# Seven smaller products for three of the seven block products in the second MLP stage, with weight low parts kept in DRAM

## The chip, the cores and the metric

The kernel runs on one core of a Trainium2 chip. The metric is the device time of one execution in microseconds (us). Here P means a tile of 128 partitions. TensorE multiplies a 128x128 weight tile (stationary) with up to 512 columns (moving) into a PSUM bank; VectorE (DVE), ScalarE (ACT) and GpSimd (POOL) prepare operands in SBUF; SyncE (SP) issues the transfers.

## The reference

```python
def _attn_ref(q, k, v):            # 8 batches, 12 heads, 448 positions, 64 per head
    scores = scale * np.matmul(q, k.transpose(0, 1, 3, 2)) - np.log(S)
    attn = 1.0 / (1.0 + np.exp(-scores))
    return np.matmul(attn, v)

def _moe_ref(x, w_in, w_out):      # x 3584 x 768, w_in 768 x 2048, w_out 2048 x 768
    h = x @ w_in
    r = np.maximum(h, 0.0)
    g = r * r
    return g @ w_out
```

Inputs and outputs are float32. The attention output, heads side by side, is `x`.

## The kernel before

The attention is computed first, pair of heads by pair of heads, and written to a DRAM scratch `xd`. On the side the MLP weights are converted and stored to `w1` and `w2` in DRAM, each as seven blocks: the sums and single blocks that a Strassen-Winograd scheme needs.

The MLP works on four groups of tokens, g = 0 to 3. Group 0 to 2 hold two halves of 512 tokens, group 3 two halves of 256. In each group `gemm1` makes the hidden activations and `gemm2` the output. Both halve all three dimensions (tokens, model width, hidden width) and compute seven block products in place of eight. In `gemm2` the block products run in the order 1, 2, 6, 7, 5, 4, 3 (`ORDER`); one is a 384 x 1024 weight block times 1024 x 512 activations.

Every float32 product is made of three passes over operands split in a high and a low part (high x high, high x low, low x high; `product`, line 613). A block product of `gemm2` is so 3 output tiles (e) x 8 hidden tiles (i) x 3 passes = 72 matmuls of 512 columns. They accumulate in PSUM banks "a", "b" or "c" (`CHAIN`): products 1, 6, 5, 3 go on in the same three banks, 7 and 4 in another three, 2 in a third three, and snapshots between them give the sums (`finish`, line 844).

What a block product needs beforehand:
- Weights. A unit is two hidden tiles of one block (128 x 768 words). `fetch` (line 650) loads it from `w1` or `w2`; `halve` (line 658) splits it: ScalarE casts the high part (line 373), VectorE subtracts it from the raw word to leave the low part (line 375). There are 7 buffers of 6 KB per partition for units. A fetch is placed 9 steps ahead of the first use, a halve 5 steps (a step is one i of one block product).
- Activations. `operand(n, j)` (line 776) makes the operand of product n for the pair j of hidden tiles: for n = 6, 7 and 4 one VectorE subtraction (lines 780, 784, 787; the last two in place), then the split, a ScalarE cast and a VectorE subtraction of 128 x 1024. It is called in every other step of the product before. All these tiles come from one set of 32 buffers of 4 KB per partition (`N2`, `flat2`): 16 hold the four blocks of squared activations, 4 the differences `gt2`, and two (high, low) are taken for every operand pair until its matmuls are over. Attention and x tiles use the same 32.
- A second set of 18 buffers of 2 KB (`N1`, `op1`) holds snapshots, outputs and the third part of the x operands.

The attention and the first `gemm1` are issued in the order in which they are written (`manual_schedule`). Everything behind it, so all `gemm2`, is ordered by the scheduler of the framework: an engine's order is its own, ready work may be taken ahead of work that waits, and the order is fixed before the run. During the `gemm2` stages GpSimd has nothing to do.

Of the kernel before, what the change touches and what calls it, by code (L numbers as in the profile page):

```python
# [9 lines left out]
F32 = mybir.dt.float32  # L10
F32R = mybir.dt.float32r
# [79 lines left out]
ORDERS = [(n, i) for n in ORDER for i in range(NI)]  # L91
LAST = ORDER[-1], -1

LOAD_AHEAD, HALVE_AHEAD = 9, 5
READY, HALVED = 5, 2

DEFERRED = (4, 5, 6, 7)
# [9 lines left out]
def sigmoid_attention_relu2_mlp(  # L107
# [7 lines left out]
    xd: bass.AP,  # L115
    w1: bass.AP,
    w2: bass.AP,
):


# [37 lines left out]
    def flat2(name, dtype=F32):  # L158
        return sb.tile([P, 2 * WIDE], dtype, tag="op2", bufs=N2, name=name)
# [12 lines left out]
    def op1(name, n, dtype=F32):  # L172
        return sb.tile([P, WIDE], dtype, tag="op1", bufs=N1, name=name)[:, :n]
# [93 lines left out]
        out.append((at + 13, store))  # L267
        return out

    def load_weights(src, name, spare=False):  # L270
# [12 lines left out]
    def halve_weights(w, later=None):  # L283

        hi, lo = w
        split_to(hi, lo, lo.bitcast(F32), later)
# [107 lines left out]
    def split_or_joint(raw, name, n):  # L394
        return joint(raw, name, 2 * WIDE // n, n) if n < WIDE else split(raw, name, n)
# [253 lines left out]

    def fetch(unit):  # L650
        g, m, i, u = unit
        if m == 0:
# [3 lines left out]
        loaded[unit] = load_weights(src, f"w{m}_{g}_{i}_{u}", unit in spare)  # L656

    def halve(unit, later=None):
        halve_weights(loaded[unit], later)

    spare = set()
    for at_unit, unit in enumerate(units):
        ahead, use = 0, first_use[unit]
        if unit[0] == NG - 1 and use >= sequence.index((NG - 1, 0, *STEPS[1][0])) + 4:
            ahead = 4
            if at_unit % 3 == 0:
                spare.add(unit)
        if at_unit >= READY:
            stream.setdefault(max(use - LOAD_AHEAD - ahead, 0), []).append((fetch, unit))
        if at_unit >= HALVED:  # L670
            stream.setdefault(max(use - HALVE_AHEAD - ahead // 2, 0), []).append((halve, unit))


    def gemm1(g, ops):
# [95 lines left out]
    def gemm2(g, blocks, operands1):  # L770
        n_tok = WIDTHS[g]
        of = 2 * WIDE // n_tok
        banks, snaps = {}, {}
        ops, t2 = {1: operands1}, {}

        def operand(n, j):

            if n == 6:
                t2[j] = blocks_of(f"gt2_{g}_{j}", n_tok)
                nc.vector.tensor_sub(out=t2[j], in0=blocks["22", j], in1=blocks["12", j])  # L780
                raw = t2[j]
            elif n == 7:
                raw = blocks["11", j]
                nc.vector.tensor_sub(out=raw, in0=t2[j], in1=raw)
            elif n == 4:
                raw = blocks["21", j]
                nc.vector.tensor_sub(out=raw, in0=raw, in1=t2[j])
            else:
                raw = blocks[{2: "21", 5: "12", 3: "22"}[n], j]
            ops.setdefault(n, {})[j] = split_or_joint(raw, f"o{n}_{g}_{j}", n_tok)  # L790

        def rest_of(e):
            t = snaps["rest", e] = op1(f"r_{g}_{e}", n_tok)
# [67 lines left out]

        def step(n, at):
            k, i = CHAIN[n], at
            if n in (1, 7, 2) and i == 0:
# [125 lines left out]
```

## Time and profile before

| | us |
|---|---|
| median of 3 runs (1055.05 to 1055.75) | 1055.62 |
| the profiled execution, its own time | 1054.56 |
| its span | 1052.8 |
| attention and first weights | about 245 |
| `gemm1`, `gemm2` of groups 0 to 2 | 114.2 each |
| group 3, both | 121.8 |

| engine | busy us of the span |
|---|---|
| TensorE | 1048.7 (100%) |
| VectorE | 806.7 (77%) |
| ScalarE | 662.5 (63%) |
| GpSimd | 73.5 (7%) |

In the rows below a time stands first where the row is one of a timeline or of the chain; `xN` is a count of instructions, `oa`, `ob`, `oc` are the PSUM banks of `gemm2`, `ha` and so on those of `gemm1`; `o_0h`, `o_0l` the high and low part of an operand of group-wise block pairs, `gt`, `g` activations, `w` a weight unit. The granted TensorE clock is 1.00 in every window.

### The profile page before, as it was taken

The page shows a single profiled execution, that of the slowest core. Times are in us where ns is not written, and L with a number is a line of the kernel's source. Part 1 is how long each engine was busy: PE and PEld are TensorE (multiplying, and loading weights), DVE is VectorE, ACT ScalarE, POOL GpSimd, SP SyncE. Part 2 cuts the span into 40 slices and gives each one's busy share as a digit, 9 for nine tenths or more (in the row PEclk, how much of TensorE's full clock was granted, in tenths as well). Part 3 has the DMA queues.
Part 4 walks back from the last instruction along what each step waited for, and adds up shares of the span by engine and source line. Part 5 has one row for each costly group of instructions (what it writes and reads, how often), then busy time and mean ns, then how long its engine had stood idle before and what let it go on. Part 6 is the DMA issues. An engine that isn't in the chain of part 4 may idle for free.

```text
span 1052.8 us, 16322 instructions
## 1 busy us (share of the span) xinstructions
PE 1048.7 (100%) x6202; PEld 812.3 (77%) x6202; DVE 806.7 (77%) x1025; ACT 662.5 (63%) x922; POOL 73.5 (7%) x44
## 2 busy tenths in 40 slices
PE   9999999999999999999999999999999999999998
PEld 4555555557888888888888888888888888899987
DVE  5999999877778899953455998834557997557997
ACT  7988988977667856634344656433344665357873
POOL 1322231200222000000000000000000000000000
PEclk9999999999999999999999999999999999999999
DMA  9999999993567535644333345543333345555662
GB/s 358 403 375 384 340 406 360 328 318 121 191 209 248 163 109 175 186 133 118 92 90 103 106 134 191 150 148 81 100 98 106 105 135 165 180 189 165 202 199 87
DMA packets 99407, 203.98 MB, mean 194 GB/s; under 512 B 9216, under 2 KB 61184, under 8 KB 99328
## 3 DMA queue, kind: packets, MB, share of 16 engines
q1 hardware_dynamic: 99184, 202.87, 58.5%
q8 instruction: 49, 0.80, 0.3%
q14 instruction: 30, 0.25, 0.1%
q10 hardware_dynamic: 144, 0.07, 0.0%
HBM read 158.86 MB, written 44.04 MB: 193 GB/s over the span
## 4 chain that ended last, share of the span: by engine, by line
PE 100%; DVE 0%; issue 0%
PE ha L617 22%; PE oa L617 19%; PE pav L347 11%; PE hb L617 9%; PE ob L617 9%; PE sc L316 9%; PE hc L617 5%; PE oc L617 5%; PE oa L625 2%; PE sr L332 2%; PE pav L359 2%; PE ob L625 1%; PE hb L625 1%; PE oa L628 1%; PE hb L628 1%; PE ob L628 1%
## 5 line engine op out<-in xcount | busy, mean ns | idle before, releaser
L375 DVE TENSOR_TENSOR w<-w 128x768 fp32r<-128x768 f32 (+1 forms) x220 | 200.1, 913 | 154.8 <-ACT w L373 153.7
L373 ACT CAST w<-w 128x768 fp32r<-128x768 f32 (+1 forms) x221 | 174.1, 793 | 176.3 <-DMA w<-w 169.1
L304 ACT ACTIVATE at<-sc 128x896 f32<-128x896 f32 x144 | 119.2, 943 | 3.2 <-PE sc L316 3.2
L347 PE MATMUL pav<-at,v 64*64 64x448 f32 x1152 | 118.1, 540 | 0.1
L347 PEld LDWEIGHTS pav<-at,v 64*64 64x64 f32 x1152 | 42.0, 133 | 60.7 <-issue 53.2
L712 ACT COPY s<-ha 128x512 f32<-128x512 f32 (+1 forms) x64 | 34.0, 532 | 80.3 <-PE ha L617 74.6
L583 DVE TENSOR_TENSOR ql<-x,qh 128x896 fp32r<-128x896 f32 x46 | 67.9, 1516 | 0.0
L208 POOL TENSOR_TENSOR a<-a,f 128x768 int32<-128x768 int32 x24 | 52.9, 2204 | 159.0 <-DVE a L205 93.9
L316 PE MATMUL sc<-qh 64*128 64x448 f32 x282 | 53.9, 379 | 0.0
L316 PE MATMUL sc<-ql,qh 64*128 64x448 f32 x282 | 51.3, 360 | 0.0
L316 PE MATMUL sc<-qh,ql 64*128 64x448 f32 x282 | 51.2, 360 | 0.0
L369 DVE TENSOR_TENSOR xo<-pav,xo 128x448 f32<-128x448 f32 x48 | 29.1, 620 | 23.5 <-ACT xo L365 21.7
L617 PE MATMUL oa<-o_3h,w 128*128 128x512 f32 x144 | 46.3, 389 | 0.0
L617 PE MATMUL oa<-o_1h,w 128*128 128x512 f32 x144 | 46.3, 389 | 0.0
L617 PE MATMUL oa<-o_0h,w 128*128 128x512 f32 x144 | 46.3, 389 | 0.0
L617 PE MATMUL oa<-o_2h,w 128*128 128x512 f32 x144 | 46.3, 389 | 0.0
L617 PE MATMUL ha<-x_0h,w 128*128 128x512 f32 x128 | 44.7, 390 | 0.0
L617 PE MATMUL ha<-x_1h,w 128*128 128x512 f32 x128 | 44.6, 389 | 0.0
L617 PE MATMUL ha<-x_2h,w 128*128 128x512 f32 x128 | 44.6, 389 | 0.0
L316 PEld LDWEIGHTS sc<-qh 64*128 64x128 f32 x282 | 26.4, 184 | 18.5 <-PE pav L347 16.2
L365 ACT COPY xo<-pav 128x448 f32<-128x448 f32 x48 | 25.5, 532 | 22.8 <-PE pav L359 11.1
L697 DVE SCALAR_TENSOR_TENSOR g<-g 128x1024 f32<-128x1024 f32 x30 | 36.9, 1230 | 0.7
(365 smaller groups left out, 2642.8 us busy)
## 6 DMA issues: line engine op xcount, KB each, us to landing
w<-w SPq DMA_DIRECT2D x192, 384.0 KB, 3.3
x<-qk SPq DMA_DIRECT2D x47, 448.0 KB, 6.2
f<-w_in SPq DMA_DIRECT2D x16, 768.0 KB, 8.8
v<-v SPq DMA_DIRECT2D x24, 448.0 KB, 6.9
xd<-xo SPq DMA_DIRECT2D x48, 224.0 KB, 5.4
w<-s SPq DMA_DIRECT2D x48, 192.0 KB, 7.5
outT<-o SPq DMA_DIRECT2D x36, 256.0 KB, 2.5
w<-a SPq DMA_DIRECT2D x12, 576.0 KB, 8.8
```

What stands on the lines that cost most here:

```text
L208: nc.gpsimd.tensor_tensor(out=wb, in0=wb, in1=t.bitcast(I32)[:, :, 0], op=ALU.add)
L304: nc.scalar.activation(at, sc, AF.Sigmoid, bias=NEG_LOG_S, scale=SCALE)
L316: nc.tensor.matmul(sc[:, j], x[kp][rows, 1, ks], x[qp][rows, 0], start=(n == 0), stop=(n == len(passes) - 1),)
L347: nc.tensor.matmul(sums[columns, h], vt[rows, n % 2 * NT + t, columns], at[t][rows, j], start=(t == 0 and (n % 2, h) != (1, 1)), stop=(t = ...
L373: nc.scalar.copy(out=hi, in_=raw)
L375: nc.vector.tensor_sub(out=lo, in0=raw, in1=hi.bitcast(F32))
L583: nc.vector.tensor_sub(out=xs[n][1], in0=x[n], in1=xs[n][0].bitcast(F32))
L617: nc.tensor.matmul(out, a[:, c], b, start=first and n == 0, stop=last and n == 2, skip_group_check=True)
L625: nc.tensor.matmul(out, w[0][:, c], x, start=first, stop=False, skip_group_check=True)
L628: nc.tensor.matmul(out[:, :n], w[1][:, c], x[:, :n], start=False, stop=last, skip_group_check=True)
L697: nc.vector.scalar_tensor_tensor(out=t, in0=t, scalar=0.0, in1=t, op0=ALU.max, op1=ALU.mult)
L712: nc.scalar.copy(out=s, in_=banks[chain, i])
```

## The change

In groups 1 and 2 the block products 2, 7 and 4 of `gemm2` (`TWICE`, `TWICE_IN`) are split again. Of their three output tiles, two (e = 0, 1) are taken together with the two hidden tiles of a pair and the two halves of 256 tokens as a 2x2x2 problem, and computed by seven products of 256 columns (`products`), accumulated in seven half banks (`SUMS_AT`). The third output tile is computed as before. What this needs:
- the sums of the weight blocks, made once in group 0 by GpSimd from the raw words (`weight_sums`, four operations of 128 x 128 per unit), split by ScalarE and VectorE, and stored to DRAM (`s2`); groups 1 and 2 load them;
- the differences of the activations, made by GpSimd (`differences_of`, four operations of 128 x 256 per pair), and their split, a ScalarE cast and a VectorE subtraction of 128 x 1024;
- the sums at the end (`add_up`), on VectorE and ScalarE, from PSUM.

Beside it, the low parts of all `gemm2` weight units are stored to DRAM in group 0 (`h2`, `keep`); in groups 1 and 2 a unit is loaded as raw words and low part, in two transfers, and only the ScalarE cast is left of its split.

```diff
+TWICE = (2, 7, 4)
+TWICE_IN = (1, 2)
+Q = WIDE // 2
+SUMS_AT = {2: (0, 0), 3: (0, 1), 4: (1, 0), 5: (1, 1), 1: (2, 0), 6: (2, 1), 7: (3, 0)}
...
-        nc.sync.dma_start(out=lo.bitcast(F32), in_=src)
+        nc.sync.dma_start(out=(lo if low is None else hi).bitcast(F32), in_=src)
+        if low is not None:
+            nc.sync.dma_start(out=lo.bitcast(F32), in_=low)
...
+        if m == 1 and u in TWICE and g <= TWICE_IN[-1]:
+            if both:
+                summed[unit] = tuple(op1(f"s{m}_{g}_{i}_{u}{c}", WIDE, F32R) for c in "hl")
+                for c, t in enumerate(summed[unit]):
+                    nc.sync.dma_start(out=t.bitcast(F32), in_=s2[i, TWICE.index(u), :, c])
+            else:
+                raw_sums[unit] = op1(f"s{m}_{g}_{i}_{u}", WIDE)
+                weight_sums(loaded[unit][1].bitcast(F32), raw_sums[unit])
...
     def halve(unit, later=None):
-        halve_weights(loaded[unit], later)
+        if unit[1] == 1 and unit[0] in TWICE_IN:
+            hi = loaded[unit][0]
+            nc.scalar.copy(out=hi, in_=hi.bitcast(F32))
+        else:
+            halve_weights(loaded[unit], later)
+
+    def keep(unit):
+        g, m, i, u = unit
+        nc.sync.dma_start(out=h2[i, u - 1], in_=loaded[unit][1].bitcast(F32))
...
+            split_to(h, l, t)
+            for c, t in enumerate((h, l)):
+                nc.sync.dma_start(out=s2[i, TWICE.index(u), :, c], in_=t.bitcast(F32))
...
             ops.setdefault(n, {})[j] = split_or_joint(raw, f"o{n}_{g}_{j}", n_tok)
+            if n in twice:
+                differences[n, j] = differences_of(raw, f"d{n}_{g}_{j}")
+
+        def differences_of(raw, name):
+
+            t, hi, lo = flat2(name), flat2(name + "h", F32R), flat2(name + "l", F32R)
+            t1, t2, t3, t4 = (t[:, k * Q : k * Q + Q] for k in range(4))
+            b11, b12, b21, b22 = (raw[:, k, h * Q : h * Q + Q] for k in range(2) for h in range(2))
+            nc.gpsimd.tensor_tensor(out=t1, in0=b12, in1=b11, op=ALU.subtract)
+            nc.gpsimd.tensor_tensor(out=t2, in0=b22, in1=t1, op=ALU.subtract)
+            nc.gpsimd.tensor_tensor(out=t3, in0=b22, in1=b12, op=ALU.subtract)
+            nc.gpsimd.tensor_tensor(out=t4, in0=b21, in1=t2, op=ALU.subtract)
+            split_to(hi, lo, t)
+            return hi, lo
...
+            for k, ((wh, wl), (xh, xl)) in operands.items():
+                at, half = SUMS_AT[k]
+                out = banks["q", at][:, half * Q : half * Q + Q]
+                for c, (a, b) in enumerate(((wh, xh), (wh, xl), (wl, xh))):
+                    nc.tensor.matmul(
+                        out, a, b, start=j == 0 and c == 0 and half == 0, stop=j == NI // 2 - 1 and c == 2,
+                        skip_group_check=True,
+                    )
...
+            if n in twice:
+                if i == 0:
+                    for e in range(4):
+                        banks["q", e] = bank(f"oq{n}_{g}_{e}", WIDE, 3 if e < 2 else None)
+                    if n != 4:
+                        banks[k, NE - 1] = bank(f"o{k}_{g}", WIDE)
+                j = i // 2
+                if i == 2 * j:
+                    products(n, j)
+                else:
+                    for c in range(2):
...
+                        product(banks[k, NE - 1], w, NE - 1, x, n != 4 and (j, c) == (0, 0), (j, c) == (NI // 2 - 1, 1))
+                if i == NI - 1:
+                    finish_twice(n)
+                after = ORDER.index(n) + 1
+                if after < len(ORDER) and i % of == 0:
+                    operand(ORDER[after], i // of)
+                return
```

## Rows read from the trace of the kernel before

**Rows 1.** The page: busy time of each engine, and the chain of waits that ended last by engine.

```profile
PE 1048.7 (100%) x6202; PEld 812.3 (77%) x6202; DVE 806.7 (77%) x1025; ACT 662.5 (63%) x922; POOL 73.5 (7%) x44
...
PE 100%; DVE 0%; issue 0%
```

**Rows 2.** The chain of waits in order of time, in `gemm2` of group 1: start us, length us, what. The first four block products (1, 2, 6, 7).

```profile
588.24 16.32 PE oa L617 x72
604.56 16.32 PE oc L617 x72
620.88 16.32 PE oa L617 x72
637.20 16.32 PE ob L617 x72
```

**Rows 3.** The timeline of TensorE in group 3, where matmuls have 256 columns: start us, length us. Between the two rows shown the timeline has 8 more single matmuls of the first row's form, all of 0.28 us.

```profile
958.55 0.28 PE L617 MATMUL ha<-x_3h,w_2h 128*128 128x256 f32 x1
...
959.63 0.86 PE L625 MATMUL hc<-x_3j,w 128*128 128x512 f32 x3
```

**Rows 4.** Busy time of each engine by window: the attention, `gemm2` of group 0, `gemm1` of group 1, `gemm2` of groups 1 and 2.

```profile
core 0: us, PE busy (x) PEld busy (x) DVE busy (x) ACT busy (x) POOL busy (x), PEclk, DMA share, GB/s
0.00:245.00 245.00, 244.12 (x2402) 136.09 (x2402) 210.60 (x282) 211.65 (x278) 53.10 (x28) 1.00 0.95 353
...
359.76:474.00 114.24, 114.24 (x505) 94.60 (x505) 96.21 (x100) 68.14 (x84) 0.00 (x0) 1.00 0.50 155
474.00:588.24 114.24, 114.24 (x505) 94.59 (x505) 62.37 (x74) 48.73 (x71) 0.00 (x0) 1.00 0.36 101
588.24:702.50 114.26, 114.26 (x505) 94.61 (x505) 94.54 (x98) 63.88 (x80) 0.00 (x0) 1.00 0.49 148
...
816.72:931.00 114.28, 114.28 (x506) 94.64 (x506) 86.00 (x91) 60.36 (x78) 0.00 (x0) 1.00 0.46 141
```

**Rows 5.** The same view by block product, group 1: products 7, 5 and 4.

```profile
637.20:653.52 16.32, 16.32 (x73) 13.51 (x73) 11.66 (x12) 9.20 (x13) 0.00 (x0) 1.00 0.70 226
653.52:669.84 16.32, 16.32 (x73) 13.51 (x73) 15.58 (x16) 9.86 (x12) 0.00 (x0) 1.00 0.49 154
669.84:686.16 16.32, 16.32 (x73) 13.51 (x73) 11.61 (x16) 5.92 (x9) 0.00 (x0) 1.00 0.55 170
```

**Rows 6.** Groups of VectorE instructions (busy us, mean ns of one): the low parts of weight units in `gemm2` of group 1, and an addition from PSUM of 256 columns (group 3).

```profile
L375 DVE TENSOR_TENSOR w<-w 128x768 fp32r<-128x768 f32 x29 | 27.6, 953 | 16.4 <-ACT w L373 15.6 <-PE oa L617 0.7
...
L716 DVE TENSOR_TENSOR g<-hc,s 128x256 f32<-128x256 f32 x8 | 3.3, 418 | 0.5 <-ACT w_0h L373 0.5
```

**Rows 7.** Timelines of ScalarE and VectorE in `gemm2` of group 1: the first cast for product 2, the first and third cast for product 7, and two subtractions for product 4 (start us, length us of all in the row).

```profile
588.94 1.04 ACT L373 CAST o_0h<-g 128x1024 fp32r<-128x1024 f32 x1
...
616.81 1.05 ACT L373 CAST o_0h<-g 128x1024 fp32r<-128x1024 f32 x1
...
621.30 1.05 ACT L373 CAST o_2h<-g 128x1024 fp32r<-128x1024 f32 x1
...
615.41 2.35 DVE L787 TENSOR_TENSOR g<-g,gt 128x1024 f32<-128x1024 f32 x2
```

**Rows 8.** Timelines of GpSimd and of VectorE where they meet, in the attention and in the first `gemm1`: first GpSimd, then VectorE.

```profile
20.46 2.58 POOL L208 TENSOR_TENSOR a<-a,f 128x768 int32<-128x768 int32 x1 [20.02 <-DVE a L205]
26.19 1.87 POOL L208 TENSOR_TENSOR a<-a,f 128x768 int32<-128x768 int32 x1 [3.14 <-DVE a L205]
...
276.20 1.62 POOL L208 TENSOR_TENSOR b<-b,fd 128x384 int32<-128x384 int32 x1 [2.99 <-issue]
...
350.52 1.03 POOL L208 TENSOR_TENSOR b<-b,fd 128x384 int32<-128x384 int32 x1 [4.64 <-DVE b L205]
...
20.24 3.75 DVE L583 TENSOR_TENSOR ql<-x,qh 128x896 fp32r<-128x896 f32 x2
...
31.00 2.08 DVE L583 TENSOR_TENSOR ql<-x,qh 128x896 fp32r<-128x896 f32 x2
...
275.99 0.95 DVE L375 TENSOR_TENSOR w<-w 128x768 fp32r<-128x768 f32 x1
...
350.90 1.72 DVE L375 TENSOR_TENSOR o_1l<-g,o_1h 128x1024 fp32r<-128x1024 f32 x1
...
356.61 1.21 DVE L375 TENSOR_TENSOR o_2l<-g,o_2h 128x1024 fp32r<-128x1024 f32 x1
```

**Rows 9.** The longest wait of the transfer queue (us in total, times, longest us), and the issues of weight units (KB each, median us from issue to landing).

```profile
SPq L280 <- PE oa L617: 143.1, 46, 3.7
...
w<-w SPq DMA_DIRECT2D x192, 384.0 KB, 3.3
```

**Rows 10.** `gemm2` of group 0: the first low part for product 7 on the timeline of VectorE, and product 7 in the chain of waits.

```profile
393.18 1.21 DVE L375 TENSOR_TENSOR o_0l<-g,o_0h 128x1024 fp32r<-128x1024 f32 x1
...
408.72 16.32 PE ob L617 x72
```

More of the change, by code (lines that the diff above doesn't have):

```diff
@@ L92 @@
 LAST = ORDER[-1], -1
-LOAD_AHEAD, HALVE_AHEAD = 9, 5
+TWICE = (2, 7, 4)
+TWICE_IN = (1, 2)
+Q = WIDE // 2
+SUMS_AT = {2: (0, 0), 3: (0, 1), 4: (1, 0), 5: (1, 1), 1: (2, 0), 6: (2, 1), 7: (3, 0)}
+LOAD_AHEAD, HALVE_AHEAD, KEEP_AFTER = 9, 5, 3
 READY, HALVED = 5, 2
@@ L117, in sigmoid_attention_relu2_mlp @@
     w2: bass.AP,
+    h2: bass.AP,
+    s2: bass.AP,
 ):
@@ L268, in deferred, with load_weights @@
         return out
-    def load_weights(src, name, spare=False):
+    def load_weights(src, name, spare=False, low=None):
         count = src.shape[1]
@@ L651, in fetch @@
         g, m, i, u = unit
+        both = m == 1 and g in TWICE_IN
         if m == 0:
@@ L655, in fetch, with weight_sums @@
             src = w2.rearrange("i p n c -> n p i c")[PLACE[1][u]][:, 2 * i : 2 * i + 2]
-        loaded[unit] = load_weights(src, f"w{m}_{g}_{i}_{u}", unit in spare)
-    def halve(unit, later=None):
-        halve_weights(loaded[unit], later)
+        loaded[unit] = load_weights(src, f"w{m}_{g}_{i}_{u}", unit in spare, h2[i, u - 1] if both else None)
+        if m == 1 and u in TWICE and g <= TWICE_IN[-1]:
[6 more added lines that the diff above has]
+                weight_sums(loaded[unit][1].bitcast(F32), raw_sums[unit])
+    summed, raw_sums = {}, {}
+    def weight_sums(raw, to):
+        a11, a12, a21, a22 = (raw[:, k, e * P : e * P + P] for e in range(2) for k in range(2))
+        s1, s2, s3, s4 = (to[:, n * P : n * P + P] for n in range(4))
+        nc.gpsimd.tensor_tensor(out=s1, in0=a21, in1=a22, op=ALU.add)
+        nc.gpsimd.tensor_tensor(out=s2, in0=s1, in1=a11, op=ALU.subtract)
+        nc.gpsimd.tensor_tensor(out=s3, in0=a11, in1=a21, op=ALU.subtract)
+        nc.gpsimd.tensor_tensor(out=s4, in0=a12, in1=s2, op=ALU.subtract)
+    def halve(unit, later=None):
+        if unit[1] == 1 and unit[0] in TWICE_IN:
[6 more added lines that the diff above has]
+        nc.sync.dma_start(out=h2[i, u - 1], in_=loaded[unit][1].bitcast(F32))
+        if unit in raw_sums:
+            t = raw_sums.pop(unit)
+            h, l = (op1(f"s{m}_{g}_{i}_{u}{c}", WIDE, F32R) for c in "hl")
+            split_to(h, l, t)
+            for c, t in enumerate((h, l)):
+                nc.sync.dma_start(out=s2[i, TWICE.index(u), :, c], in_=t.bitcast(F32))
     spare = set()
@@ L671, in sigmoid_attention_relu2_mlp @@
             stream.setdefault(max(use - HALVE_AHEAD - ahead // 2, 0), []).append((halve, unit))
+        if unit[:2] == (0, 1):
+            stream.setdefault(use - HALVE_AHEAD + KEEP_AFTER, []).append((keep, unit))
     def gemm1(g, ops):
@@ L774, in gemm2 @@
         ops, t2 = {1: operands1}, {}
+        twice = TWICE if g in TWICE_IN else ()
+        differences = {}
         def operand(n, j):
@@ new lines, in products, with block, total, part @@
+        def products(n, j):
+            unit = g, 1, j, n
+            w, s, d = loaded[unit], summed[unit], differences[n, j]
+            def block(e, k):
+                return tuple(t[:, k, e * P : e * P + P] for t in w)
+            def total(k):
+                return tuple(t[:, k * P - P : k * P] for t in s)
+            def part(k, h):
+                return tuple(t[:, k, h * Q : h * Q + Q] for t in ops[n][j])
+            def difference(k):
+                return tuple(t[:, k * Q - Q : k * Q] for t in d)
+            operands = {
+                2: (block(0, 1), part(1, 0)),
+                3: (total(4), part(1, 1)),
+                4: (block(1, 1), difference(4)),
+                5: (total(1), difference(1)),
+                1: (block(0, 0), part(0, 0)),
+                6: (total(2), difference(2)),
+                7: (total(3), difference(3)),
+            }
+            for k, ((wh, wl), (xh, xl)) in operands.items():
[6 more added lines that the diff above has]
+                    )
@@ new lines, in add_up @@
+        def add_up(n, base):
+            both = [banks["q", 0], banks["q", 1]]
+            if base:
+                outs = [op1(f"q{n}_{g}_{e}", WIDE) for e in range(2)]
+                for e in range(2):
+                    nc.vector.tensor_add(out=outs[e], in0=both[e], in1=base[e])
+                both = outs
+            ends = op1(f"qe{n}_{g}", WIDE)
+            first, second = ends[:, :Q], ends[:, Q:]
+            third = op1(f"qt{n}_{g}", Q)
+            nc.scalar.copy(out=first, in_=banks["q", 2][:, :Q])
+            nc.vector.tensor_add(out=second, in0=banks["q", 2][:, Q:], in1=first)
+            nc.vector.tensor_add(out=third, in0=banks["q", 3][:, :Q], in1=second)
+            nc.vector.tensor_add(out=second, in0=banks["q", 1][:, Q:], in1=second)
+            outs = outs if base else [op1(f"q{n}_{g}_{e}", WIDE) for e in range(2)]
+            nc.vector.tensor_add(out=outs[0], in0=both[0], in1=ends)
+            for h in range(2):
+                columns = slice(h * Q, h * Q + Q)
+                nc.vector.tensor_add(out=outs[1][:, columns], in0=both[1][:, columns], in1=third)
+            return outs
@@ new lines, in finish_twice @@
+        def finish_twice(n):
+            if n == 7:
+                for e, t in enumerate(add_up(n, None)):
+                    snaps[7, e] = t
+                snap(7, NE - 1, "b")
+                return
+            if n == 4:
+                for e in range(2):
+                    nc.vector.tensor_add(out=snaps[2, e], in0=snaps[2, e], in1=snaps[7, e])
+            r = (0, NE)[n == 4]
+            for e, o in enumerate(add_up(n, [snaps[1 if n == 2 else 2, e] for e in range(2)])):
+                at = STARTS[g]
+                nc.sync.dma_start(out=outT[(r + e) * P : (r + e + 1) * P, at : at + n_tok], in_=o)
+            finish(n, NE - 1)
@@ L863, in step @@
             k, i = CHAIN[n], at
+            if n in twice:
[9 more added lines that the diff above has]
+                    for c in range(2):
+                        w = tuple(t[:, c].rearrange("p (c m) -> p c m", m=P) for t in loaded[g, 1, j, n])
+                        x = tuple(t[:, c] for t in ops[n][j])
+                        product(banks[k, NE - 1], w, NE - 1, x, n != 4 and (j, c) == (0, 0), (j, c) == (NI // 2 - 1, 1))
[4 more added lines that the diff above has]
+                    operand(ORDER[after], i // of)
+                return
             if n in (1, 7, 2) and i == 0:
@@ L983 @@
     args.append(nc.dram_tensor("outT", (DM, B * S), F32, kind="ExternalOutput").ap())
-    for n, shape in (("xd", (NP, P, B * S)), ("w1", (NI, P, 7, HALF)), ("w2", (NI, P, 7, HALF))):
+    scratch = {
+        "xd": (NP, P, B * S),
+        "w1": (NI, P, 7, HALF),
+        "w2": (NI, P, 7, HALF),
+        "h2": (NI // 2, 7, P, 2, HALF),
+        "s2": (NI // 2, len(TWICE), P, 2, WIDE),
+    }
+    for n, shape in scratch.items():
         args.append(nc.dram_tensor(n, shape, F32, kind="Internal").ap())
```

## The prediction

> **What bounds the kernel now.** I read the busy times first, then the chain of waits, then the windows stage by stage, and last the timelines of the engines that feed TensorE. TensorE is busy all the time and alone on the chain that ended last [rows 1]: there is no wait to remove, and only less work on it makes the kernel faster. In `gemm2` each block product takes 16.32 us for 72 matmuls of 512 columns, so 226.7 ns for one, and the next begins where it ends [rows 2]. The windows tell how near the others are: in `gemm2` of group 1 VectorE is busy 94.5 of 114.3 us, ScalarE 63.9, GpSimd 0; in group 2 VectorE 86.0; in the `gemm1` between them 62.4 [rows 4]. So TensorE sets the time, with VectorE not far behind in just the stages that change.
>
> A second thing must be seen. The first cast for product 2 starts at 588.94, right behind the end of `gemm1` at 588.24; the first for product 7 at 616.81 is 12.25 us into product 2, which is three of its four pairs (12.24); the third at 621.30 follows the end of product 2 at 620.88 [rows 2, 7]. The casts wait for buffers that TensorE gives back: the 32 of 4 KB are all in use.
>
> **The change part by part.** *Matmuls.* In group 3 nine matmuls of 256 columns, each with its own weight load, take 959.63 - 958.55 = 1.08 us, 120 ns each [rows 3]. A pair in a changed product had 12 matmuls of 512 columns for the two output tiles, 12 x 226.7 = 2.72 us; it gets 21 of 256, 21 x 120 = 2.52 us. The third tile stays (6 x 226.7 = 1.36). A pair goes from 4.08 to 3.88 us, a product from 16.32 to 15.52. Six products: 6 x 0.80 = 4.8 us less. An eighth fewer columns would be 0.32 us per pair (768 at the granted 2.4 GHz); 0.12 of it go to the 13.3 ns that a matmul takes beyond its columns (226.7 - 213.3, 120 - 106.7), nine times more.
>
> The Trainium skill (TensorE: Matmul & The Clock Gate, Back-to-back issue gap) gives for streams of weight load and matmul some 131 ns at 512 columns and 81 at 128; my estimate from it is 98 ns at 256, by which a pair would go from 1.57 to 2.06 us and the change would cost 24 x 0.48 = 12 us. The rows have the same pairs of load and matmul at 226.7 and 120 ns, and decide; I give this no chance.
>
> *VectorE.* Of the 29 low parts of units in the window [rows 6] 28 are the group's own and go: at 953 ns 26.7 us less, some 24 at the pace at which they follow each other. Added are 12 low parts of differences of 128x1024, 1.14 us each (two such take 2.35 [rows 7], so 2.35 - 1.21 [rows 8] = 1.14 apart): 13.7 us. The additions behind products 2, 7 and 4 come to about 20 of 0.4 to 0.7 us from PSUM [rows 6], less the six that go: some 9 us. By itself that is even: 94.5 - 24 + 14 + 9 = 94.
>
> *GpSimd, and what it does to VectorE.* 48 operations of 128x256 in each group. Alone, 128x768 takes 1.87 and 128x384 1.03 us; 256 columns are then 0.75. But they do not run alone. At 20.46 GpSimd started within the first of two VectorE subtractions: the two took 3.75 us, undisturbed 2.08, and GpSimd 2.58 in place of 1.87. At 276.20, behind a subtraction that had begun at 275.99, 384 columns took 1.62 in place of 1.03. At 350.90 a subtraction under a GpSimd operation took 1.72 in place of 1.21 [rows 8]. A VectorE instruction with both inputs in SBUF and one of GpSimd so exclude each other: 768 columns hold VectorE off for 1.67 us, 384 for 350.52 + 0.88 (it should have ended 1.21 after a start, so started at 351.41). By these two, 256 columns hold 0.62 us. Where VectorE always has an instruction ready they alternate, one GpSimd operation every 0.62 + 1.14 = 1.76 us, and the four of a pair take 7.0; where VectorE is idle 4 x 0.75 = 3.0. I take 7.0 for the stretch below, since VectorE is busy in 94.5 of 114 us before the holds, and 94 + 48 x 0.62 = 124 us of work against 111.9 of TensorE leaves it no idle time.
>
> The Trainium skill (SBUF — State Buffer, Who interferes with whom) has the two share a port pair that one holds for its whole instruction. By that 0.75 instead of 0.62 would be held, a pair would take 7.6 us, and the stretch below would end 1.2 us later per group, 1063.8 in all; the rows show VectorE going on 0.1 us before GpSimd's recorded end.
>
> *Where it ends on the path: product 7.* Its operands are made while product 6 runs. Let 0 be the start of product 6. Of the 32 buffers 16 hold blocks, 4 `gt2` and 8 the operands of product 6: 4 are free, product 6 gives back 2 every 4.08 us (4.08 to 16.32), product 7 then 4 for each pair done. A pair of product 7 now takes 5, in this order: high, low, raw differences, their high and low; two come back when it is ready (the raw one and the block's). Pair 0: GpSimd from about 1 to 8, then cast 1.05, a hold of 0.62, subtraction 1.22: ready at 10.9. Pair 1: raw buffer at 8.2, GpSimd to 15.2, ready 18.1. Pair 2: raw buffer only at 16.3, GpSimd to 23.4, ready 26.3. Pair 3: GpSimd from 23.4 to 30.4, ready 33.3. They are due at 16.32 + 3.88 j: 16.3, 20.2, 24.1, 28.0. Pairs 0 and 1 are in time, pair 2 is 2.2 us late and pair 3 5.3. TensorE so waits 5.3 us in product 7 of each group, 10.6 in two. If pair 1 must take the raw buffer that pair 0 gives back (10.9), the same steps end 9.9 us late; with GpSimd alone nothing is late: 0 to 9.9 per group are the bounds. Products 2 and 4 have the same work, but before 2 the blocks are ready and VectorE runs out of work, and before 4 the buffers are free early: 0, within the same bounds.
>
> *Group 0.* 48 GpSimd operations of 128 columns hold VectorE some 0.36 us each, 17 us, and 12 splits of 0.6 add 7: 120 against 114.2 us [rows 4]. Product 7's first low part is ready 15.5 us ahead of its product [rows 10], so I cost it at 0; if that cover goes, up to 6 us.
>
> *Transfers.* Group 1 moves 16.9 MB in `gemm2` (114.3 us at 148 GB/s); low parts add 28 x 0.39 = 11.0, sums 12 x 0.52 = 6.3. Products 7, 5 and 4 are the worst: 9.0 MB before [rows 5] and 17.9 after in 47.4 us, 377 GB/s where the attention ran at 353 [rows 4]: 3.3 us behind. Units wait for one of 7 buffers that TensorE gives back [rows 9], so they land about 6 x 4.08 - 3.3 = 21 us ahead: cost 0, bound 3.3 per group. ScalarE (63.9 + 12 x 1.05) and PSUM (eight banks, each read a product before it is needed) cost nothing.
>
> Sum: -4.8 + 10.6 = +5.8 against the profiled 1054.56 us (span 1052.8 and 1.8 around it), so 1060.4. The median is 1.06 above that execution: **1061.4**.
>
> **The rivals.** *GpSimd slips in between.* The 28 units that leave VectorE leave gaps, GpSimd's operations fall into them, and a pair takes under 4.4 us: then pair 3 is ready at 16.3 + 2 x 4.4 + 2.9 = 28.0, in time, TensorE never waits, and the time is 1055.62 - 4.8 = **1050.8**. For it: nothing added to VectorE is urgent but the low parts, and the scheduler may put them first. Against: the 124 us above. *Half of it*: 1 to 3.5 us late per group, 1053.5 to 1057.7. *VectorE behind as a whole*: 124 against 111.9 us in group 1, and 94 - 8.5 + 30 = 115 in group 2, cannot be pushed into the next `gemm1` since its x operands come last; all of both late, and group 0's 6: 1055.62 - 4.8 + 12 + 3 + 6 = 1072. *Transfers decide*: 1055.62 - 4.8 + 6.6 = 1057.4. That the change does not do what it says would be 256 columns at over 129.5 ns (2.72 / 21); rows 3 exclude it.
>
> **How the numbers follow.** Product 7 late by 3.5 to 10 us per group: 0.46, its own range 1057.7 to 1071. No wait: 0.30. One group only, net gain over 0.2%: 0.04. Half of it: 0.12. VectorE as a whole: 0.05. Transfers: 0.03. A measurement here tells 0.2% (2.1 us) from no change. Faster 0.34, same 0.14 (half of it, and part of the transfers), slower 0.52. The range goes from the clean gain less 0.5 to the top of the likeliest, 1050.3 to 1071; VectorE as a whole and the edges are left out.
>
> **What would show it.** Right: changed products at 15.52 us in the chain where nothing waits; waits of TensorE in product 7, for VectorE's low parts, in its later pairs, in both groups; GpSimd at 1.2 us and more for 256 columns; VectorE near 100% there. Wrong: a chain with TensorE alone and a span shorter by 4.8 us; or GpSimd at 0.75.

## The result, and the profile after

Measured together, the kernel before took 1055.68 us and the changed one 1067.15 us (medians; 1063.49 to 1069.48 over four runs for the changed one): a ratio of 1.0108, 95% interval 1.0067 to 1.0148. The change makes the kernel 11.5 us slower; 1061.4 was predicted, with a range of 1050.3 to 1071. One run of the kernel before, at 2742.31 us, and one of `e8`, at 3754.89, stand far apart from all others and do not enter the ratios. The profiled execution of the changed kernel took 1069.48 us, the slowest of the four, with a span of 1067.7: what the stages lose below is more than what the median loses.

The page of the changed kernel, busy time and the chain of waits by engine:

```profile
PE 1051.8 (99%) x6418; PEld 821.5 (77%) x6418; DVE 835.4 (78%) x1045; ACT 687.9 (64%) x960; POOL 241.7 (23%) x188
...
PE 81%; DVE 9%; DMA 3%; ACT 2%; POOL 2%; issue 2%; SPq 0%; ACTq 0%; DVEq 0%; POOLq 0%
```

TensorE is no longer alone on the chain, as it was in [rows 1]. Where the time went is read best by stage: the time from the first matmul of one stage to the first of the next, in the two profiled executions, and the term that the prediction had for it.

| stage | before, us | after, us | change | predicted |
|---|---|---|---|---|
| attention, `gemm1` and `gemm2` of group 0 | 473.84 | 474.23 | +0.39 | 0 |
| `gemm1` of group 1 | 114.24 | 120.29 | +6.05 | 0 |
| `gemm2` of group 1 | 114.24 | 114.57 | +0.33 | +2.9 |
| `gemm1` of group 2 | 114.24 | 118.69 | +4.45 | 0 |
| `gemm2` of group 2 | 114.24 | 114.87 | +0.63 | +2.9 |
| group 3 | 121.97 | 125.02 | +3.05 | 0 |
| sum | 1052.77 | 1067.66 | +14.9 | +5.8 |

10.5 of the 14.9 us stand where nothing was predicted: in the first 14 us of the `gemm1` stages behind group 0 and behind group 1.

**The changed products.** The chain of waits in `gemm2` of group 1 of the changed kernel, start us, length us, what; first a pair of product 2, then product 7 with its last waits:

```profile
611.00 2.51 PE oq L883 x21
613.51 1.39 PE oc L626 x6
...
626.60 16.32 PE oa L626 x72
642.91 2.53 PE oq L883 x21
...
649.33 1.65 POOL d L846
...
654.42 0.74 POOL d L849
...
655.19 1.06 ACT d_3h L382
...
656.27 1.37 DVE d_3l L384
...
657.68 1.94 PE oq L883 x14
659.62 1.39 PE ob L626 x6
661.00 16.32 PE oa L626 x72
```

A pair takes 2.51 + 1.39 = 3.90 us, the 21 matmuls of 256 columns 119.5 ns each. Product 7 runs from 642.91 to 661.00, 18.09 us in place of 15.60. On its chain stands just what was predicted: the four GpSimd operations of the last pair, the cast, the subtraction on VectorE. Where TensorE stood is on its timeline:

```profile
652.12 0.38 PE L883 MATMUL oq<-d_2l,w 128*128 128x256 f32 x1 [0.58 <-DVE d_2l L384]
...
657.68 0.38 PE L883 MATMUL oq<-d_3l,w 128*128 128x256 f32 x1 [1.01 <-DVE d_3l L384]
```

These are the third and the fourth pair. It is the same two in group 2 (885.7 and 891.2 us), where product 7 takes 18.35 us.

**The start of `gemm1` of group 1.** Its chain of waits, and then TensorE's timeline and windows at the same place:

```profile
469.61 5.98 DMA w<-w
...
475.67 0.84 ACT w L382
...
478.19 0.48 ACT o L951
...
478.69 2.02 DMA outT<-o
...
480.82 0.59 ACT s L757
```

```profile
478.08 0.39 PE L626 MATMUL hc<-y_1h,w 128*128 128x512 f32 x1
481.45 0.79 PE L626 MATMUL ha<-x_1h,w 128*128 128x512 f32 x1 [2.99 <-ACT s L757]
482.05 0.63 PE L626 MATMUL ha<-x_1l,w 128*128 128x512 f32 x1
482.47 1.05 PE L626 MATMUL ha<-x_1h,w 128*128 128x512 f32 x2
```

```profile
core 0: us, PE busy (x) PEld busy (x) DVE busy (x) ACT busy (x) POOL busy (x), PEclk, DMA share, GB/s
...
481.50:485.70 4.20, 4.20 (x10) 3.33 (x11) 1.19 (x3) 0.83 (x1) 0.00 (x0) 0.50 0.66 237
```

A weight unit lands late, and so the casts behind it are late, the last output copy of group 0, its store, and the 2 KB buffer that the store gives back. Into that buffer ScalarE copies `ha` (line 757) so that TensorE may go on. TensorE waits 2.99 us, and then its granted clock is 0.50, the 1.2 GHz level, in the whole window shown and on to about 487.2: matmuls follow each other by 0.42 us (482.05 to 482.47) in place of 0.23. About half of the 6.05 us is wait and half is clock. Why the unit is late: the stores of the kept low parts (line 696) and of the outputs (line 952) stand in the one queue with the loads, and wait for VectorE. SyncE's waits in group 0 of the changed kernel (us in total, times, longest), and then one of VectorE's in the same stretch:

```profile
SPq L696 <- DVE w L384: 26.1, 11, 3.8
SPq L952 <- DVE o L949: 16.9, 9, 6.7
```

```profile
DVE w L384 <- POOL s L685: 9.8, 9, 2.4
```

The last row has VectorE wait for GpSimd: the low part of a unit is written over the raw words that GpSimd's sums read, so it cannot be made before the sums. The last four of these waits, 7.0 us together, lie between 431 and 444 us, and from 444 to 476 VectorE is busy in 32.0 of 32.0 us.

**The start of `gemm1` of group 2.** Its chain of waits:

```profile
704.81 0.60 DVE q L904
...
705.74 0.60 DVE yx L439
...
713.30 1.15 DVE x L439
...
714.47 0.62 ACT x_2h L382
...
715.42 0.61 ACT y_2h L382
716.03 0.49 ACT s L757
```

VectorE's additions behind product 4 (line 904) and the x operands of the next group (lines 439, 384) follow each other almost without a gap through the last product of `gemm2`: its busy time there was 6.79 us of 16.32 before (first row) and is 16.26 after (second row):

```profile
686.16:702.48 16.32, 16.32 (x73) 13.51 (x73) 6.79 (x9) 5.78 (x10) 0.00 (x0) 1.00 0.43 134
```

```profile
692.92:709.24 16.32, 16.32 (x74) 13.51 (x73) 16.26 (x23) 12.86 (x18) 0.00 (x0) 1.00 0.81 297
```

The casts of x wait for it on ScalarE, and behind them in ScalarE's order the copy of `ha`: TensorE waits 2.79 us, and here too its granted clock is 0.50 behind the wait (716.57 to 718.00), up to about 719.4. Some 2.9 of the 4.45 us are the wait, the rest is clock.

Part of VectorE's backlog is time in which it stood still. The last loads of x stand in SyncE's queue behind an output store that waits 9.0 us for VectorE (first row: us in total, times, longest), and VectorE then stands idle 4.47 us for the first of them (second row):

```profile
SPq L952 <- DVE o L949: 12.4, 3, 9.0
```

```profile
685.55 1.23 DVE L439 TENSOR_TENSOR x<-x,x 128x1024 f32<-128x1024 f32 x1 [4.47 <-DMA x<-xd]
```

### The profile page after: what moved, and what is told of

It is laid out like the page before. It is cut to its first block, busy times and chain, and to the rows that moved or that the text cites. A ratio compares the mean times of both kernels' runs of the same rounds, so it can differ in the third digit from the quotient of the medians.

```text
span 1067.7 us, 17202 instructions
## 1 busy us (share of the span) xinstructions
PE 1051.8 (99%) x6418; PEld 821.5 (77%) x6418; DVE 835.4 (78%) x1045; ACT 687.9 (64%) x960; POOL 241.7 (23%) x188
## 4 chain that ended last, share of the span: by engine, by line
PE 81%; DVE 9%; DMA 3%; ACT 2%; POOL 2%; issue 2%; SPq 0%; ACTq 0%; DVEq 0%; POOLq 0%
PE ha L626 20%; PE oa L626 14%; PE pav L356 11%; PE hb L626 9%; PE sc L325 9%; PE hc L626 4%; PE oq L883 3%; PE ob L626 3%; PE oc L626 2%; DMA w<-w 2%; PE sr L341 2%; PE pav L368 2%; DVE w L384 1%; POOL d L846 1%; DVE gt L827 1%
## 5 line engine op out<-in xcount | busy, mean ns | idle before, releaser
L384 DVE TENSOR_TENSOR w<-w 128x768 fp32r<-128x768 f32 (+1 forms) x164 | 148.5, 913 | 95.7 <-ACT w L382 82.1
L382 ACT CAST w<-w 128x768 fp32r<-128x768 f32 (+1 forms) x165 | 127.0, 778 | 82.4 <-DMA w<-w 78.8
L846 POOL TENSOR_TENSOR d<-g 128x256 f32<-128x256 f32 x24 | 33.6, 1400 | 339.2 <-PE ha L626 283.7
L690 ACT CAST w<-w 128x768 fp32r<-128x768 f32 x56 | 46.7, 834 | 29.6 <-DMA w<-w 29.6
L215 POOL TENSOR_TENSOR b<-b,fd 128x384 int32<-128x384 int32 x16 | 20.4, 1278 | 118.8 <-ACT w L382 56.9
```

Of the source, the lines that this page charges most:

```text
L215: nc.gpsimd.tensor_tensor(out=wb, in0=wb, in1=t.bitcast(I32)[:, :, 0], op=ALU.add)
L690: nc.scalar.copy(out=hi, in_=hi.bitcast(F32))
L846: nc.gpsimd.tensor_tensor(out=t1, in0=b12, in1=b11, op=ALU.subtract)
```

## The experiments

Twelve kernels ran. The ratio is always to the kernel before on the same chip (its medians 1054.99 to 1055.34 us), with its 95% interval.

**Who makes the sums and differences.** In `e1` the differences of the activations go to VectorE, in `e2` the sums of the weights too.

```diff
-            nc.gpsimd.tensor_tensor(out=t1, in0=b12, in1=b11, op=ALU.subtract)
+            nc.vector.tensor_tensor(out=t1, in0=b12, in1=b11, op=ALU.subtract)
...
-        nc.gpsimd.tensor_tensor(out=s1, in0=a21, in1=a22, op=ALU.add)
+        nc.vector.tensor_tensor(out=s1, in0=a21, in1=a22, op=ALU.add)
```

> The four differences of a pair (128x256) are made by VectorE in place of GpSimd; all else as in the changed kernel. Exclusion (GpSimd operations hold VectorE off and are held off by it): 48 holds of 0.62 us per group become 48 instructions of 0.33 us, no alternation; the waits of TensorE in product 7 (2.5 and 2.75 us) go, and so does most of the waits at the start of the gemm1 of group 2 and of group 3 (4.5 and 3.1), which come from VectorE's backlog; the one at the start of group 1's gemm1 (6.0) stays: 1055 to 1059. Transfers (the kept low parts fill the queue): only product 7's waits go: 1061 to 1063. Buffers alone (32 of 4 KB): product 7's waits stay: 1065 and more.

> As the run before, and the weight sums of group 0 (128x128) are on VectorE too, so that GpSimd does nothing in any gemm2. Exclusion: the wait at the start of group 1's gemm1 (6.0 us with the lower clock behind it) shrinks too, as VectorE is held off by 48 x 0.36 = 17 us less and has 48 x 0.2 = 10 us more: 1051 to 1055. Transfers: that wait stays, since stores of low parts and sums are as many as before: no better than the run before it, 1056 to 1062.

`e1`: 1065.80 us, 1.0102 (1.0077 to 1.0128), 7 us above its forecast. `e2`: 1059.06 us, 1.0041 (1.0026 to 1.0056), in the range of the theory of transfers, though the wait that this theory wanted to stay is gone. Moving the weight sums gave 6.7 us, and most of it by stage is here: `gemm1` of group 1 takes 119.69 us in `e1` and 114.24 in `e2`. Moving the differences took most of the loss in `gemm1` of group 2 away (115.03 in `e1`) and made `gemm2` of group 2 faster than before, 113.74 us, but that of group 1 slower, 117.07 (`e2` 118.43). There product 7's second pair is late. ScalarE's timeline in `e2`:

```profile
641.67 0.83 ACT L690 CAST w<-w 128x768 fp32r<-128x768 f32 x1 [4.16 <-DMA w<-w]
642.41 1.04 ACT L382 CAST d_1h<-d 128x1024 fp32r<-128x1024 f32 x1
```

The cast of the differences stands behind the cast of a unit that waits 4.16 us for its load, although the differences were ready at 641.2. TensorE waits 1.99 us there, and its granted clock is 0.50 from 645 to 647 us, so part of the 118.43 is clock.

**The two parts apart.** `e3` keeps the low parts in DRAM and leaves all block products as before; `e4` has the smaller products without kept low parts.

```diff
-TWICE = (2, 7, 4)
+TWICE = ()
```

```diff
-        loaded[unit] = load_weights(src, f"w{m}_{g}_{i}_{u}", unit in spare, h2[i, u - 1] if both else None)
+        loaded[unit] = load_weights(src, f"w{m}_{g}_{i}_{u}", unit in spare, None)
...
-        if unit[1] == 1 and unit[0] in TWICE_IN:
-            hi = loaded[unit][0]
-            nc.scalar.copy(out=hi, in_=hi.bitcast(F32))
-        else:
-            halve_weights(loaded[unit], later)
+        halve_weights(loaded[unit], later)
...
-        nc.sync.dma_start(out=h2[i, u - 1], in_=loaded[unit][1].bitcast(F32))
```

> The low parts are kept and loaded as in the changed kernel, but no product is split in seven (no sums, no differences, no GpSimd in gemm2). Exclusion: no loss, VectorE has 24 us less per group: 1055 to 1056, as before the change. Transfers: stores of the low parts in group 0 stand in the transfer queue ahead of the units for group 1's gemm1, and this wait of some 6 us stays: 1060 to 1063.

> The three products are split in seven as in the changed kernel, but the low parts are made by VectorE in every group, not kept. Exclusion: 24 us more on VectorE in the gemm2 of groups 1 and 2, which has none to spare: waits in product 7 and at the next gemm1 grow, 1072 to 1085. Transfers: 11 MB less to store in group 0 and to load in 1 and 2; the waits at the start of the gemm1s (6.0, 4.5, 3.1) go: 1054 to 1058.

`e3`: 1055.06 us, 0.9999 (0.9990 to 1.0009), every stage as before. `e4`: 1089.26 us, 1.0323 (1.0308 to 1.0339); `gemm2` of group 1 takes 129.38 us, of group 2 122.55, with waits for low parts all through product 7; that is more than either theory forecast. The kept low parts cost nothing and gain nothing alone; what they do is make room on VectorE for the rest.

The two bear on `gemm1` of group 1 as well. In `e3` the stores of the low parts wait for VectorE in group 0 for longer than in the changed kernel, and the stage is as before:

```profile
SPq L696 <- DVE w L384: 44.1, 18, 5.9
```

In `e4`, with GpSimd's sums and without these stores, the stage takes 115.66 us, against 120.29 in the changed kernel. So the full loss takes both, the stores in the queue and the sums on GpSimd.

**Without the differences.** `e6` leaves the differences of the activations out (the smaller products take the operand's own parts); matmuls, transfers and additions stay, and the weight sums are on VectorE.

```diff
-                differences[n, j] = differences_of(raw, f"d{n}_{g}_{j}")
+                differences[n, j] = ops[n][j]
```

> The differences of the activations are left out (the smaller products take the operand's own high and low parts in their place); weight sums on VectorE, as in e2_all_on_vector. Matmuls, transfers, kept low parts and the additions at the end stay. Theory (the matmuls gain 0.80 us per product, 4.8 us in all, and what eats it hangs on the making of the differences): gemm2 of groups 1 and 2 at 111.0-112.2 us each, time 1050.2-1052 us. Rival (transfers, the sums' loads among them, delay product 7 by themselves): gemm2 of group 1 at 114 us or more, time 1053-1058 us.

1052.74 us, 0.9978 (0.9968 to 0.9989), 0.7 us above the forecast of its theory. Its chain of waits in `gemm2` of group 1 has TensorE alone, here at product 7:

```profile
619.75 16.32 PE oa L626 x72
636.07 2.51 PE oq L883 x21
638.58 1.39 PE ob L626 x6
...
651.67 16.32 PE oa L626 x72
```

Both `gemm2` take 112.08 us, 2.16 less than before: the matmuls give 0.72 us per product, and the transfers, all still there, delay none. What is lost hangs on the differences. Only group 3 is 2.1 us longer than before, behind a late weight unit (wait of 1.18 us at 934.9).

**The weight sums alone.** `e7` has the sums on VectorE, the differences on GpSimd (the second half of the diff of `e2`).

> As the changed kernel, with the weight sums of group 0 on VectorE alone and the differences still on GpSimd. Theory (GpSimd in group 0 holds VectorE, whose late low parts hold the kept stores in SyncE's queue and so the next unit loads): the stage behind group 0 falls from 120.3 to 114.2-114.5 us, all else stays, time 1060-1062 us. Rival (the stores themselves delay the loads): it stays near 120 us and the time at 1066-1068 us.

1064.08 us, 1.0079 (1.0063 to 1.0094). `gemm1` of group 1 is back at 114.24 us: with the sums off GpSimd the loss goes, as forecast, though the median stays 2 us above the forecast, for `gemm2` of group 1 gets longer, 115.40. VectorE's own work in group 0 grows. Windows of the changed kernel and of `e7`:

```profile
360.00:474.20 114.20, 114.20 (x505) 94.58 (x504) 101.78 (x104) 69.70 (x90) 42.50 (x48) 1.00 0.86 299
```

```profile
360.00:474.20 114.20, 114.20 (x506) 94.56 (x505) 110.04 (x158) 72.64 (x95) 0.00 (x0) 1.00 0.87 307
```

VectorE goes from 101.78 to 110.04 us of 114.20, and the loss is gone. So it was not VectorE's sum of work that made the stores late; it was GpSimd beside it. GpSimd acts in two ways there: it holds VectorE off while both run, and VectorE waits 9.8 us for its sums, a wait that `e7` does not have. Which of the two counts, and how much lies in the order that the scheduler made anew, no run tells apart.

**The queue of the sums' loads.** `e5` is `e2` with the loads of the weight sums issued by GpSimd.

```diff
-                    nc.sync.dma_start(out=t.bitcast(F32), in_=s2[i, TWICE.index(u), :, c])
+                    nc.gpsimd.dma_start(out=t.bitcast(F32), in_=s2[i, TWICE.index(u), :, c])
```

> All subtractions on VectorE as in e2_all_on_vector (1059.06 us), and the loads of the weight sums issued by GpSimd, which has nothing else to do, in place of SyncE. Theory (in group 1 of e2 the sums' loads, which wait for their own buffers in SyncE's queue, hold the unit loads behind them back; the cast of a late unit then holds the cast of product 7's differences on ScalarE): gemm2 of group 1 falls from 118.4 to 112.5-114 us, the time to 1053-1055 us. Rival (VectorE has too much to do in group 1, whatever the queue): gemm2 of group 1 stays at 117-119 us and the time at 1058-1060 us. Rival (transfers are at their limit in products 7 and 4): the same, 1058-1060 us, with unit loads that take as long from issue to landing as in e2.

1066.36 us, 1.0108 (1.0088 to 1.0128): outside all its forecasts, 7 us worse than `e2`. `gemm2` of group 1 takes 120.77 us and of group 2 119.75, with waits from product 7's first pair on. Product 7's first pair waits here for VectorE's low part, not for a cast behind a late unit. Since it is another pair that is late first, whether the unit loads hold product 7 in `e2` stays open. VectorE's timeline of `e5` has no pause from the additions behind product 2, at 624.70, to 643.95, and the first pair's low part begins only at 637.98. With everything on VectorE, it is full just there; that the order of its work, which the scheduler fixes anew for each kernel, decides what is late is argued, not shown.

**Which products.** `e8` has products 2 and 4 as smaller products and product 7 as before, sums on VectorE, differences on GpSimd; `e9` is the same with the differences on VectorE; `e10` has product 2 alone, as `e8`.

```diff
-TWICE = (2, 7, 4)
+TWICE = (2, 4)
```

> Only products 2 and 4 as smaller products, product 7 as before; weight sums on VectorE, differences on GpSimd, as in e7_sums_on_vector (1064.08 us). By e6_no_differences a changed product is worth 0.72 us where nothing waits. Theory (as predicted for the change: the operands of product 7 alone come late, those of 2 and 4 have cover): gemm2 of groups 1 and 2 at 112.7-113.0 us, all gemm1 at 114.2-114.5, time 1051.5-1053.5 us. Rival (what GpSimd takes from VectorE is made up for later, whichever product it is made for, in the casts at the start of the next gemm1): gemm1 of group 2 stays at 117-119 us though gemm2 itself is clean, time 1055-1060 us.

> As e8_products_2_4, with the differences on VectorE too. Theory (in e2 it is product 7's operands that VectorE makes too late, in products 6 and 7): gemm2 of both groups at 112.7-113.0 us, gemm1 at 114.2-114.5, time 1051.5-1053.5 us. Rival (VectorE full in all of gemm2): waits in product 4, gemm2 at 114-117 us, time 1055-1058 us.

> Only product 2 as smaller products; weight sums on VectorE, differences on GpSimd. Theory (product 2's operands are made with VectorE work to spare): gemm2 of groups 1 and 2 at 113.5 us, gemm1 at 114.2-114.5, time 1053.2-1054.5 us. Rival (GpSimd's hold of VectorE reaches through to the next gemm1 from there too): gemm1 of group 2 at 116 us or more, time 1055.5-1058 us.

`e8`: 1053.34 us, 0.9982 (0.9973 to 0.9991). `e9`: 1053.04 us, 0.9979 (0.9970 to 0.9988). `e10`: 1054.19 us, 0.9993 (0.9984 to 1.0002). In `e8` and `e9` both `gemm2` take 112.80 us and every other stage of groups 0 to 2 114.24 to 114.43; in `e10` 113.52. That is 0.72 us per product, twice and once, without a wait, and with GpSimd or VectorE alike. All three theories hold, and the rival falls: GpSimd's work for products 2 and 4 reaches through to no `gemm1`. `e8` and `e9`, whose intervals overlap, are the fastest complete kernels here, 0.2% under the one before.

**The buffers of product 7.** `e11` is `e7`, and `e12` is `e2`, with the differences written into the buffer of their low part and split there: four buffers of 4 KB for a pair in place of five.

```diff
-            t, hi, lo = flat2(name), flat2(name + "h", F32R), flat2(name + "l", F32R)
-            t1, t2, t3, t4 = (t[:, k * Q : k * Q + Q] for k in range(4))
+            hi, lo = flat2(name + "h", F32R), flat2(name + "l", F32R)
+            t1, t2, t3, t4 = (lo[:, k * Q : k * Q + Q] for k in range(4))
...
-            split_to(hi, lo, t)
+            split_to(hi, lo, lo.bitcast(F32))
```

> As e7_sums_on_vector (1064.08 us), with the differences written into the buffer of their low part and split there, so that a pair of product 7 takes four buffers of 4 KB in all and not five (the differences are rounded on the way, so their low parts hold nothing; no instruction is left out). Theory (the want of buffers makes product 7 late: in e7 the second pair's differences stand 6 us for the buffer that the first operand's low part gives back): no wait over 0.5 us in product 7, gemm2 of groups 1 and 2 at 112.1-113.2 us, gemm1 of group 2 at 114.2-115.5, time 1053-1057 us. Rival (GpSimd and VectorE in each other's way, with the additions behind product 2 in front, set the pace, whatever the buffers): gemm2 at 114.5-116 us, gemm1 of group 2 at 118-119.5, time 1062-1065 us.

> As e2_all_on_vector (1059.06 us), with the differences in the buffer of their low part, as in e11_in_place. Theory (buffers): gemm2 of groups 1 and 2 at 112.1-113.2 us, time 1051.5-1054 us, no slower than with products 2 and 4 alone. Rival (the order in which late unit loads and casts stand on ScalarE and SyncE makes product 7's second pair late, as in e2): gemm2 of group 1 at 115-118.5 us, time 1056-1060 us.

`e11`: 1058.66 us, 1.0033 (1.0023 to 1.0044), some 5 us under `e7`. GpSimd's timelines in product 6 of group 1, the end of the first pair and the start of the second, in `e7` and then in `e11`:

```profile
622.61 1.60 POOL L849 TENSOR_TENSOR d<-g,d 128x256 f32<-128x256 f32 x1
630.24 5.00 POOL L846 TENSOR_TENSOR d<-g 128x256 f32<-128x256 f32 x1 [6.03 <-DVE o_0l L384]
```

```profile
623.40 1.61 POOL L849 TENSOR_TENSOR d_0l<-g,d_0l 128x256 fp32r<-128x256 f32 x1
624.97 0.74 POOL L846 TENSOR_TENSOR d_1l<-g 128x256 fp32r<-128x256 f32 x1
```

The second pair no longer waits 6 us, and `gemm2` goes from 115.40 to 113.23 us in group 1 and from 114.85 to 112.57 in group 2, with no wait over 0.5 us in product 7: here the buffers were the cause. But `gemm1` of group 2 stays at 117.57 us, with its copy of `ha` 3.04 us late, not far from the rival's 118 to 119.5; the time lies between the two forecasts. `e12`, 1056.14 us, 1.0010 (1.0001 to 1.0019), is the other way round: `gemm1` of group 2 clean at 114.37 us, but waits of 0.5 to 0.9 us for VectorE's low parts in product 7 of both groups, 115.03 and 113.67 us. The time is in the rival's range, but the waits are not for a cast behind a late unit load, as the rival had it. Neither theory had that whole: one buffer less and VectorE alone remove different parts of the loss, and no kernel here has all three products and no wait.

## Why the prediction was right, and where it was not

The direction and the range hold, and so does the mechanism on which it was built, that product 7's operands come late because GpSimd and VectorE exclude each other. But of the 19.2 us that the profiled execution lost against a clean gain (14.9 + 4.3), only 5.2 come from the place where it put the loss. With that loss alone the change would have cost 0.9 us (5.2 - 4.3), no change that a measurement here can tell, and not 5.8. That the kernel is slower, and near the forecast, it owes to three places that the prediction had put at nothing: in this it was luck.

**Matmuls: right, the gain a little small.** 21 matmuls take 2.51 us (2.52 predicted); the third tile takes 1.39 where 1.36 was reckoned, so a product gains 0.72 us and not 0.80, six 4.3 and not 4.8. The Trainium skill (TensorE: Matmul & The Clock Gate, Back-to-back issue gap), by which the prediction estimated 98 ns at 256 columns, does not agree with this trace: 119.5 ns, and the rows at hand decided rightly.

**VectorE even without the holds: right.** In `gemm2` of group 1 of `e6` VectorE is busy 81.4 us; with 12 low parts of differences at 1.14 it is 95, against 94 reckoned.

**GpSimd and VectorE exclude each other: right in kind, 0.54 us and not 0.62 in size.** The timelines of GpSimd and VectorE in product 7 of group 2 of the changed kernel:

```profile
882.88 1.66 POOL L846 TENSOR_TENSOR d<-g 128x256 f32<-128x256 f32 x1 [1.16 <-DVE g L834]
884.50 1.71 POOL L848 TENSOR_TENSOR d<-g 128x256 f32<-128x256 f32 x1
...
888.66 0.74 POOL L846 TENSOR_TENSOR d<-g 128x256 f32<-128x256 f32 x1
```

```profile
883.86 1.76 DVE L384 TENSOR_TENSOR d_2l<-d,d_2h 128x1024 fp32r<-128x1024 f32 x1
885.54 1.75 DVE L384 TENSOR_TENSOR o_3l<-g,o_3h 128x1024 fp32r<-128x1024 f32 x1
```

They alternate, 1.68 us from one subtraction to the next (885.54 - 883.86) where an undisturbed one follows by 1.14; where VectorE has nothing, GpSimd takes 0.74 (at 888.66). The Trainium skill (SBUF — State Buffer, Who interferes with whom) would have a hold of the whole instruction, 0.74 us; 0.54 is measured, so here GpSimd's recorded time is longer than what it holds.

**Product 7: the right place, half the size.** With the start of product 6 at 626.60 as 0, the last pair's low part was forecast ready at 33.3 and is there at 31.1 (657.68); product 7 loses 2.5 us in group 1 and 2.75 in group 2, not 5.3, which is the size of the rival "Half of it" (1 to 3.5 us; by its own sum that gives 1052.8 to 1057.8 us, not from 1053.5). The step that was mis-sized is "the four of a pair take 7.0": the third pair's ran from 643.36 to 648.2, 4.8 us, and the fourth's from 649.33 to 655.2, 5.8, since VectorE has pauses while it waits for ScalarE's casts: it was forecast near 100% there, and is busy 16.20 of 16.31 us in product 6 but 13.96 of 18.09 in product 7. The last 0.6 us of the difference are matmuls: the fourth pair's first seven of 21 do not need the late low part (`x14` are left at 657.68 in the chain). That the want of buffers gates the pairs holds (`e11`), and that products 2 and 4 cost nothing in `gemm2` (`e8`).

**Group 0: wrong.** "Product 7's first low part is ready 15.5 us ahead of its product, so I cost it at 0." (It begins 15.5 us ahead and is ready 14.3 ahead.) The cover that counted was another: the stores of the kept low parts wait for VectorE in the one transfer queue, ahead of the loads for the next stage, and VectorE waits for GpSimd's sums, which the prediction did not see. It cost 6.05 us. The prediction's "up to 6 us" if that cover goes is the same number by chance: it was VectorE's work beyond the stage, and half of what was measured is clock. `e7`, `e3` and `e4` show that the full loss takes both, the sums on GpSimd and the stores. That the late load is the way it takes is read from the chain of the changed kernel; in `e1` that loss came by VectorE's subtractions of x and output copies without the late load.

**VectorE behind as a whole: dismissed with the wrong reason.** It "cannot be pushed into the next `gemm1` since its x operands come last". Just because they come last they are late: the casts of x and the copy of `ha` stand in ScalarE's order behind them, and `gemm1` of group 2 loses 4.45 us. `e2`, `e12` (without GpSimd) and `e8` (without product 7) bring it to 115.3, 114.4 and 114.2: most of the loss needs GpSimd's differences, and product 7 among them. Both are not enough: `e4` has them too, and 114.4 after a `gemm2` that is 15 us longer. VectorE's wait for x stands in the three kernels that lose most here (4.47 us, `e7` 4.4, `e11` 5.2) and in neither `e2` nor `e12`, but `e8` has 5.6 without a loss. How much is hold and how much the wait for x stays open.

**Transfers: right for `gemm2`.** `e6` moves all of them, and its `gemm2` of groups 1 and 2 do not wait. The stores of group 0 were not in the term, and they have a part in the loss behind it.

**Group 3, 3.05 us: not in the prediction.** Its `gemm1` waits 1.38 us at 951.6 for a weight unit that took 5.45 us to land. Its `gemm2` takes the other half, with a wait of 0.83 us for a low part at 1056.3. `e3` does not have the loss (122.2 us in all, before 121.97), every kernel with smaller products has some of it, `e6` without any differences too. What delays that load stays open.

## What to carry to other kernels

Where an engine gets more to do, look for cover at each place where its results are due, above all in the first steps of the stage behind, whose operands stand last in its order; a sum of busy time that fits the stage says nothing of these. Before work is given to GpSimd because it is idle, count what it takes from VectorE and what of VectorE's has to wait for it: here the weight sums of 12 units on GpSimd cost 6 us in the next stage and on VectorE, fuller by 8 us, nothing. A store that waits for an engine can delay the loads behind it in the same queue, as it did those of x. And split such a change by its products: the one whose operands lacked time and buffers ate the gain of the other two.

## What was not expected of the hardware

- A wait of 2.99 us at the start of `gemm1` of group 1 was followed by a granted clock of 0.50 to about 487.2, and cost 6.05 us in all; one of 2.79 us at the start of `gemm1` of group 2 likewise, 4.45 in all. In `e11` a wait of 3.04 us at the same place of group 2 was followed by 1.00 in the window 709.50 to 715.00, and cost 3.33. What tells them apart was not tried.
- GpSimd does not always take its turn: in `e7` the operation at 630.24 took 5.00 us, while VectorE ran four 128x1024 subtractions one after the other.
- Where the kernel waits, its time goes with the granted clock: the changed kernel's four runs took 1063.49, 1065.61, 1068.70 and 1069.48 us at a mean granted clock of 0.999, 0.998, 0.997 and 0.995. So most of the clock's part of the loss in the profiled run is missing in the fastest. `e9`, which has next to no waits, had 0.999 or 1.000 in all eleven and stays within 1.5 us (1051.85 to 1053.32).
